# Hand-placed attention units and shared output parts in a fused attention + SwiGLU kernel

## The chip, the cores and the metric

One core of one Trainium2 chip. The metric is device time in microseconds (us) of one execution. Most executions of one kernel agree within a per cent (the four of before: 264.87 to 266.14); those that are over 1.5% above the fastest of the same kernel are marked slow and left out of the ratios.

The engines by their names in the profile: PE is the matrix engine (TensorE), PEld its weight loads, DVE the vector engine, ACT the scalar engine, POOL GpSimd, SP the sync engine, which here issues DMAs; SPq is its queue.

## The reference

Sliding-window attention with sink tokens, followed by RMS norm and a SwiGLU feed-forward network (FFN), on 4 x 768 tokens. Cut to what matters:

```python
# q, k, v: (4 batches, 8 heads, 768 positions, 64), float32; n_sink = 4, window = 128
keep = is_sink | ((rel >= 0) & (rel < window))            # rel = query position - key position
a = softmax(where(keep, q @ k.T / sqrt(64), -1e9))
x = concat_heads(a @ v)                                   # (3072, 512)

xn = x / sqrt(mean(x * x) + 1e-6) * rms_g
g  = xn @ w_gate                                          # (512, 1536)
out = (g * sigmoid(g) * (xn @ w_val)) @ w_out             # (1536, 512), float32 out
```

## The kernel before

The 3072 tokens are 24 blocks of 128 (6 for each batch), and 6 *groups* of 4 blocks. The FFN runs a group at a time. Its work is a list of *parts*: for each of 12 slices of the hidden size one gate part and one value part (four matmuls of 512 columns each), then 12 output parts of four matmuls (three for each of the group's four blocks). So a whole group has 36 parts. One part takes PE 0.863 us by the spacing of its matmuls in the trace.

Between the parts the kernel sets *attention units* of blocks to come. For block g these are, in order: scores (`unit_s`), the product with v (`unit_attend`), and for every second block an RMS chain (`unit_rms`: eight small DVE operations) that ends in two scaled blocks `xr`. From block 8 on a DMA transpose issued on SP makes `xnt` of `xr`, the layout that gate and value matmuls read. The first matmul of a group reads the `xnt` of all four of its blocks, so the last one has a deadline. From block 12 on q and k are transposed by DMA too (`qkT`), on the same SP queue. Loads of q, k, v are issued on POOL.

```python
def parts_f(G, fts, cols):
    def gate():                     # PE: pg ; ACT: th = tanh(pg / 2)
        ...
    def val():                      # PE: pvl ; DVE: p = (th + 1) * pg ; DVE: hT = p * pvl
        ...
    return [gate, val]

def parts_o(G, tb):                 # three parts; each: 4 matmuls po += hT * wo
    ...

# unit_av, the end of unit_attend:
    later(1 if g < GB else 2, lambda: unit_sq(g, u))        # ACT: sum of squares
    if u == 1 and g >= 2 and g % 2 == 1:
        later(2 if g < GB else 4, lambda: unit_rms(g))      # DVE chain, after so many parts

# the end of unit_rms:
    for i in range(2):
        unit_xr(g - 1 + i, y[:, 5, i:i + 1])                # DVE xr, then SP DMA transpose to xnt

# the driver (GB = 4 blocks a group, NG = 6 groups): units spread evenly over a group's parts
def run(parts, slots):
    n, i = len(parts), 0
    for s, f in enumerate(parts):
        while i < len(slots) and i < (s + 1) * len(slots) / n:
            for u in slots[i]:
                u()
            i += 1
        f()
        tick()                      # runs what `later` has put off

for G in range(NG):
    parts = fb[8:] if G == 0 else []
    if G > 0:
        for ft in range(FTN):
            parts += parts_f(G, (ft,), slice(0, GN))
        for tb in range(GB):
            parts += parts_o(G, tb)
    n1 = 4 * ((G + 2) * GB + 1 - 4) + (3 if G == 0 else 4)
    run(parts, slots[n:n1])
    n = n1
# [cut: prologue, attention units, loads]
```

The softmax here doesn't subtract the row's maximum and nothing guards it: scores larger than these inputs give would overflow.

## Time and profile before

| kernel before | |
|---|---|
| time, median of 4 runs | 264.96 us (264.87 to 266.14) |
| profiled execution (a run of its own, 267.6 us) | span 265.6 us, mean granted clock 0.972 |
| first gate matmul of groups 0 to 5, end of the last matmul | 17.1, 76.0, 118.2, 156.5, 195.8, 230.3, 261.6 us |
| stretches at half clock | 15.0-21.8, 35.5-38.9, 107.2-110.6 us |

First the profile page of before: busy time of each engine, the granted clock in 40 slices of the span (tenths), the chain of waits by engine, and one of the costliest groups (busy us, mean ns of one; then the idle time before its instructions, and what ended most of it).

```profile
PE 244.9 (92%) x1735; PEld 124.3 (47%) x1761; DVE 167.9 (63%) x398; ACT 139.0 (52%) x322; POOL 106.1 (40%) x145
...
PEclk9968979999999999799999999999999999999998
...
PE 58%; DVE 28%; ACT 8%; issue 4%; DMA 1%; DVEq 0%; ACTq 0%
...
L669 PE MATMUL po<-wo,hT 128*128 128x512 bf16 x279 | 66.5, 385 | 6.6 <-DVE hT L654 6.0
```

PE is the engine that bounds, but its 92% is not how close to the end it is: the matmul of 512 columns is listed at 385 ns, and four of them follow each other in 863 ns, 216 ns each, so the listed times overlap. Waits below are read from the spacing of matmuls: the start of one, less the start of the one before and what that one takes undisturbed.

The idle time of 6.0 us in the last line is the place where the change aims. The timeline of DVE and then of PE at the end of group 3 (start us, duration us, engine, line, operation, output<-inputs, form, count; in brackets the idle time before and what ended it):

```profile
180.35 0.69 DVE L654 TENSOR_TENSOR hT<-p,pvl 128x512 bf16<-128x512 bf16 x1
180.95 0.15 DVE L541 SCALAR_TENSOR_TENSOR m<-ms 128x2 f32<-128x2 f32 x1
...
182.00 0.16 DVE L563 SCALAR_TENSOR_TENSOR y<-y 128x2 f32<-128x2 f32 x1
182.20 1.41 DVE L578 SCALAR_TENSOR_TENSOR xr<-x,y,gb 128x512 bf16<-128x512 bf16 x2
183.53 0.68 DVE L646 SCALAR_TENSOR_TENSOR p<-th,pg 128x512 bf16<-128x512 bf16 x1
184.32 0.69 DVE L654 TENSOR_TENSOR hT<-p,pvl 128x512 bf16<-128x512 bf16 x1
```

```profile
181.26 2.54 PE L669 MATMUL po<-wo,hT 128*128 128x512 bf16 x11
185.06 0.39 PE L669 MATMUL po<-wo,hT 128*128 128x512 bf16 x1 [1.27 <-DVE hT L654]
```

The RMS chain and two `xr` (180.95 to 183.6) stand on DVE ahead of the last `p` and `hT`; PE has run 11 output matmuls and waits for that `hT`. The SP queue, in the same stretch:

```profile
182.98 2.50 SPq L585 DMA_TRANSPOSE xnt<-xr  x2
```

The last two transposes for group 4 are issued at 183.0 and 184.3.

### The profile page before, as it was taken

How to read it: one execution, taken by the hardware profiler on the slowest of the kernel's cores; microseconds unless marked ns; L12 is line 12 of the kernel's file. 1: busy time of each engine (PE TensorE's matmuls, PEld its weight loads, DVE VectorE, ACT ScalarE, POOL GpSimd, SP SyncE). 2: the span in 40 equal slices, each digit the busy share in tenths (PEclk: the TensorE clock that was granted, in tenths of full speed). 3: DMA queues.
4: the chain of work that ended last, by engine and by line, in shares of the span. 5: the costliest groups of instructions: out<-in, count | busy, mean ns of one | idle time of the engine just before them, and what ended most of it. 6: DMA issues, size and time to landing. Idle time of an engine off the chain costs nothing.

```text
span 265.6 us, 4787 instructions
## 1 busy us (share of the span) xinstructions
PE 244.9 (92%) x1735; PEld 124.3 (47%) x1761; DVE 167.9 (63%) x398; ACT 139.0 (52%) x322; POOL 106.1 (40%) x145
## 2 busy tenths in 40 slices
PE   7989879998999996999998998998999998999993
PEld 2546658554544442444443443443444443444441
DVE  4644757796658988317979139988139984078700
ACT  2748644789985551645662464571664431333211
POOL 8977787378999850742321100330331000000000
PEclk9968979999999999799999999999999999999998
DMA  9999999998999999696410640501221103200022
GB/s 128 153 175 191 182 155 190 174 155 88 160 148 178 141 146 87 109 158 111 88 33 20 140 121 21 83 20 33 88 79 39 3 0 80 99 22 0 0 81 79
DMA packets 108025, 26.27 MB, mean 99 GB/s; under 512 B 97249, under 2 KB 104929, under 8 KB 108002
## 3 DMA queue, kind: packets, MB, share of 16 engines
q0 software_dynamic: 80704, 13.90, 70.3%
q1 hardware_dynamic: 26258, 11.81, 21.6%
q10 hardware_dynamic: 1040, 0.26, 0.5%
q8 instruction: 14, 0.23, 0.4%
q14 instruction: 9, 0.07, 0.1%
HBM read 28.31 MB, written 6.29 MB: 130 GB/s over the span
## 4 chain that ended last, share of the span: by engine, by line
PE 58%; DVE 28%; ACT 8%; issue 4%; DMA 1%; DVEq 0%; ACTq 0%
PE po L669 17%; PE pg L628 16%; PE pvl L628 15%; DVE hT L654 7%; DVE p L646 6%; DVE xr L578 5%; ACT et L443 2%; PE pT L434 2%; ACT th L641 2%; DVE x L522 2%; PE pqk L241 2%; DVE et L409 2%; DMA osb<-in_q_dram 1%; PE pv L487 1%; PE pv L483 1%
## 5 line engine op out<-in xcount | busy, mean ns | idle before, releaser
L628 PE MATMUL pg<-xnt,wg 128*128 128x512 bf16 (+1 forms) x310 | 75.2, 364 | 3.2 <-ACT xnt L617 1.2
L628 PE MATMUL pvl<-xnt,wv 128*128 128x512 bf16 (+1 forms) x314 | 74.6, 362 | 0.4 <-DVE p L646 0.2
L641 ACT ACTIVATE th<-pg 128x512 bf16<-128x512 f32 x72 | 43.4, 602 | 56.6 <-PE pg L628 54.2
L669 PE MATMUL po<-wo,hT 128*128 128x512 bf16 x279 | 66.5, 385 | 6.6 <-DVE hT L654 6.0
L646 DVE SCALAR_TENSOR_TENSOR p<-th,pg 128x512 bf16<-128x512 bf16 x72 | 49.2, 683 | 27.6 <-ACT th L641 27.1
L654 DVE TENSOR_TENSOR hT<-p,pvl 128x512 bf16<-128x512 bf16 x72 | 49.5, 687 | 10.2 <-PE pvl L628 2.0
L411 POOL TENSOR_SCALAR_AFFINE_SELECT et<-et 128x512 bf16<-128x512 bf16 x30 | 19.5, 656 | 85.8 <-ACT et L443 77.9
L628 PEld LDWEIGHTS <-wg 128*128 128x128 bf16 x320 | 31.0, 100 | 32.4 <-issue 3.5
L669 PEld LDWEIGHTS <-hT 128*128 128x128 bf16 x288 | 27.7, 99 | 39.3 <-DVE hT L654 8.0
L628 PEld LDWEIGHTS <-wv 128*128 128x128 bf16 x320 | 31.4, 100 | 30.1 <-issue 0.3
L443 ACT ACTIVATE et<-pT 128x512 bf16<-128x512 f32 x76 | 39.4, 607 | 1.4 <-PE pT L434 1.4
L676 ACT ACTIVATE osb<-po 128x512 f32<-128x512 f32 x24 | 14.4, 600 | 47.2 <-PE po L669 47.2
L517 DVE RECIPROCAL rden<-pv 128x4 f32<-128x4 f32 x48 | 8.4, 176 | 32.5 <-PE pv L487 32.5
L123 POOL DMA_DIRECT2D v<-in_v_dram x24 | 21.8, 910 | 4.5 <-DMA wo<-in_moe_w_out_dram 2.8
L110 POOL DMA_DIRECT2D ks<-in_k_dram x23 | 20.8, 905 | 4.0 <-DMA wo<-in_moe_w_out_dram 3.1
L110 POOL DMA_DIRECT2D qs<-in_q_dram x23 | 20.9, 908 | 3.1 <-DMA wv<-in_moe_w_val_dram 2.1
L522 DVE TENSOR_TENSOR x<-pv,rden 128x256 bf16<-128x256 f32 x48 | 20.4, 424 | 1.7
L532 ACT ACTIVATE sq<-x 128x256 bf16<-128x256 bf16 x48 | 20.0, 431 | 2.0 <-DVE x L522 1.1
L416 POOL TENSOR_SCALAR_AFFINE_SELECT et<-et 128x512 bf16<-128x512 bf16 x24 | 16.0, 667 | 0.0
L578 DVE SCALAR_TENSOR_TENSOR xr<-x,y,gb 128x512 bf16<-128x512 bf16 x20 | 14.9, 785 | 0.4
L487 PE MATMUL pv<-v,et 128*128 128x65 bf16 x168 | 12.7, 194 | 1.2 <-DVE et L409 0.8
L434 PE MATMUL pT<-qkT 64*128 64x256 bf16 (+1 forms) x168 | 12.5, 262 | 0.4 <-DVE p L646 0.4
(79 smaller groups left out, 185.7 us busy)
## 6 DMA issues: line engine op xcount, KB each, us to landing
out_dram<-osb SPq DMA_DIRECT2D x24, 256.0 KB, 2.2
v<-in_v_dram POOLq DMA_DIRECT2D x24, 128.0 KB, 7.1
qs<-in_q_dram POOLq DMA_DIRECT2D x23, 128.0 KB, 6.5
ks<-in_k_dram POOLq DMA_DIRECT2D x23, 128.0 KB, 6.9
wg<-in_moe_w_gate_dram POOLq DMA_DIRECT2D x6, 256.0 KB, 8.1
wv<-in_moe_w_val_dram POOLq DMA_DIRECT2D x6, 256.0 KB, 8.2
wo<-in_moe_w_out_dram POOLq DMA_DIRECT2D x2, 768.0 KB, 11.3
osb<-in_q_dram SPq DMA_DIRECT2D x1, 256.0 KB, 3.9
```

The lines of the kernel that those rows point to most:

```text
L110: nc.gpsimd.dma_start(out=tl, in_=src[b, :, t * P:(t + 1) * P, :].rearrange("h t d -> t h d"),)
L123: nc.gpsimd.dma_start(out=V16[b][:, t, :, 0:D], in_=v[b, :, t * P:(t + 1) * P, :].rearrange("h t d -> t h d"),)
L411: nc.gpsimd.affine_select(out=ev[:, :, 0, :], in_=ev[:, :, 0, :], compare_op=ALU.is_ge, fill=0.0, base=0, pattern=[[0, x], [1, P]], channe ...
L443: nc.scalar.activation(out=et[:, hi].rearrange("p j n c -> p (j n c)"), in_=banks[u][hi], func=ACT.Exp, scale=inv_sqrt_d,)
L522: nc.vector.tensor_tensor(out=X16[g][:, heads_of(g, u), :], in0=pvv[:, :, 0:D], in1=RDEN.pop((g, u)).unsqueeze(2).to_broadcast((P, 4, D)), ...
L532: nc.scalar.activation(out=sq, in_=xh, func=ACT.Square, scale=MS_SCALE, accum_out=MS[g // 2][:, g % 2, u:u + 1],)
L578: nc.vector.scalar_tensor_tensor(out=xr, in0=x16, scalar=y, in1=gb, op0=ALU.mult, op1=ALU.mult,)
L628: nc.tensor.matmul(out=ps[:, i * n:(i + 1) * n], lhsT=w_sb[:, kt, ft * P:(ft + 1) * P], rhs=XNT[G][:, kt, cols], start=(kt == 0), stop=(kt ...
L641: nc.scalar.activation(out=st["th"], in_=st["pg"], func=ACT.Tanh, scale=0.5)
L646: nc.vector.scalar_tensor_tensor(out=p1, in0=st["th"], scalar=1.0, in1=st["pg"], op0=ALU.add, op1=ALU.mult,)
L654: nc.vector.tensor_tensor(out=HT[key][:, i:i + n, cols], in0=p1.rearrange("p (n c) -> p n c", n=n), in1=pvl.rearrange("p (n c) -> p n c", ...
L669: nc.tensor.matmul(out=st["po"], lhsT=HT[(G, ft // 2)][:, ft % 2, tb * P:(tb + 1) * P], rhs=wo[:, ft, :], start=(ft == 0), stop=(ft == FTN ...
```

## The change

Its intent: (1) fewer waits in the prologue and group 0; (2) half of a group's output parts (9 of group 0's 12 stay, 6 of the others') go between the gate and value parts of the *next* group, to thin out DVE's work there; (3) attention units at hand-picked part numbers; (4) the RMS chain in three pieces (chain, xr, xr), each put off to another part, so that the last `hT` does not wait for them. The diff, cut to its core:

```diff
-        ps = pp[0].tile([P, 512], FP32, name="pgt", tag="ph", bufs=6)   # unit_gb: RMS weights spread by
-        ...                                                             # one-row fp32 matmuls
+    nc.sync.dma_start(out=gt, in_=moe_rms_g.rearrange("(k p) -> p k", p=P))
+    # and gb by a broadcast DMA; more idle (warming) matmuls in the prologue
@@ masks of group 1's blocks on POOL, not DVE
-            dve = b < POOL_MASK_FROM or t == 0
-            wait = 0 if not dve else 1 if g < GB else 1 + 2 * u
+            wait = 0 if not by_dve(g) else 1 if g < GB else 1 + u
@@ unit_av, unit_rms
-            later(1 if g < GB else 2, lambda: unit_sq(g, u))
+            later(0 if g < GB else 1, lambda: unit_sq(g, u))
-            later(2 if g < GB else 4, lambda: unit_rms(g))
+            later(0 if g < GB else 1 if g < 2 * GB else 3, lambda: unit_rms(g))
-            unit_xr(g - 1 + i, y[:, 5, i:i + 1])
+            later(0 if g < GB else 1 if g < 2 * GB else 1 + i, lambda i=i: unit_xr(g - 1 + i, y[:, 5, i:i + 1]))
@@ loads, a group later
-    LOADS = {4: (8, 9), 5: (10, 11), 6: (12,), 7: (13, 14), 8: (15,), 9: (16, 17),
-             10: (18,), 11: (19, 20), 12: (21,), 13: (22, 23)}
+    LOADS = {8: (13, 14), 9: (15,), 10: (16, 17), 11: (18,), 12: (19, 20), 13: (21,),
+             14: (22, 23)}
@@ the driver: [cut: hand-picked part numbers for group 0]
+                for ft in range(FTN):
+                    parts += parts_f(G, (ft,), slice(0, GN))
+                    if ft % 2 == 1 and outs:
+                        parts.append(outs.pop(0))
+                for g in range(8 if G == 1 else 4 * G + 5, min(4 * G + 9, NB + 1)):
+                    p = 5.5 * (g - 8) if G == 1 else 9 * (g - 4 * G - 5)
+                    slots += step(g, p, 1.4 if g < 12 else 2)
+            outs = [p for tb in range(GB) for p in parts_o(G, tb)]
+            own = 9 if G == 0 else 6 if G < NG - 1 else len(outs)
+            parts += outs[:own]
+            outs = outs[own:]
```

`step(g, p, d)` puts the four stages of block g's units at parts p, p+d, p+2d, p+3d. It also attends block g - 1.

More of the change, by code (lines that the diff above doesn't have):

```diff
@@ L69 @@
     FA = 8
-    POOL_MASK_FROM = 1
     MANUAL = {mybir.EngineType.PE, mybir.EngineType.SP, mybir.EngineType.Pool}
@@ L154 @@
     nc.vector.memset(sel, 0.0)
-    raw = [opool.tile([P, DM], FP32, name="osb") for _ in range(3)]
+    raw = [opool.tile([P, DM], FP32, name="osb") for _ in range(2)]
     for i, src in enumerate((q, k)):
@@ L163 @@
         )
-    nc.sync.dma_start(
-        out=raw[2][0:1, :], in_=moe_rms_g.rearrange("(o d) -> o d", o=1),
-    )
-    nc.vector.memset(gb[0:1, 0:P], 1.0)
+    nc.sync.dma_start(out=gt, in_=moe_rms_g.rearrange("(k p) -> p k", p=P))
     def unit_cast(i):
@@ L172, in unit_cast @@
         (QS, KS_)[i][0] = tl
-    def unit_gb():
-        ps = pp[0].tile([P, 512], FP32, name="pgt", tag="ph", bufs=6)
-        for kt in range(KTN):
-            nc.tensor.matmul(
-                out=ps[:, kt:kt + 1], lhsT=raw[2][0:1, kt * P:(kt + 1) * P],
-                rhs=gb[0:1, 0:1], start=True, stop=True, skip_group_check=True,
-            )
-        nc.scalar.copy(out=gt, in_=ps[:, 0:KTN])
-        ps = pp[0].tile([P, 512], FP32, name="pgb", tag="ph", bufs=6)
-        nc.tensor.matmul(
-            out=ps, lhsT=gb[0:1, 0:P], rhs=raw[2][0:1, :], start=True, stop=True,
-        )
-        nc.scalar.copy(out=gb, in_=ps)
     with tc.manual_schedule(engines={mybir.EngineType.Pool, mybir.EngineType.DVE}):
@@ L231 @@
             load_v(g)
+            if g == GB + 1:
+                nc.gpsimd.memset(gb, 0.0)
         load_q(2 * GB)
+        load_k(2 * GB)
         load_wo(0)
@@ L254, in unit_t1 @@
             QKT[b] = qkt.tile([P, 2, HP, S], BF16, name="qkT")
-        ps = pp[0].tile([P, 512], FP32, name="pqk", **kind(g == 2)).bitcast(BF16)
+        ps = pp[0].tile([P, 512], FP32, name="pqk", **kind(False)).bitcast(BF16)
         transposes(ps, (QS, KS_)[i].pop(g), 0)
@@ L264, in unit_load @@
             load_q(g)
-        load_k(g)
+            load_k(g)
         load_v(g)
@@ L401, in bank, with by_dve, mask @@
         return pp[0].tile([P, 512], FP32, name="pT", tag="b1")
-    def mask(ev, b, t, nq):
+    def by_dve(g):
+        return g < GB or g % NT == 0
+    def mask(ev, g, nq):
         x = ev.shape[1]
-        if b < POOL_MASK_FROM or t == 0:
+        t = g % NT
+        if by_dve(g):
             m = masks[:, 0 if t == 0 else 1, 0:nq, :]
@@ L453, in masked @@
                 e = et if len(his) == 2 else et[:, his[0]:his[0] + 1]
-                mask(e.rearrange("p i j n c -> p (i j) n c"), b, t, nq)
-            dve = b < POOL_MASK_FROM or t == 0
-            wait = 0 if not dve else 1 if g < GB else 1 + 2 * u
+                mask(e.rearrange("p i j n c -> p (i j) n c"), g, nq)
+            wait = 0 if not by_dve(g) else 1 if g < GB else 1 + u
             for his in [(0, 1)] if nq == 2 else [(0,), (1,)]:
@@ L595, in unit_x @@
         xr = XR.pop(g)
-        n = KTN // 2 if g < GB else KTN
+        n = KTN // 2 if g < 2 else KTN
         for k0 in range(0, KTN, n):
@@ L608, in unit_x @@
                 nc.scalar.copy(out=dest, in_=src)
-            elif k0 > 0:
+            elif k0 > 0 or g == 3:
                 nc.vector.tensor_tensor(
@@ L680, in parts_o, with step @@
         return [lambda i=i: part(i) for i in range(FTN // 4)]
-    LOADS = {4: (8, 9), 5: (10, 11), 6: (12,), 7: (13, 14), 8: (15,), 9: (16, 17),
-             10: (18,), 11: (19, 20), 12: (21,), 13: (22, 23)}
-    def step(g):
+    LOADS = {8: (13, 14), 9: (15,), 10: (16, 17), 11: (18,), 12: (19, 20), 13: (21,),
+             14: (22, 23)}
+    def step(g, p, d):
         b, t = divmod(g, NT)
+        at = [p + d * i for i in range(4)]
         slots = [[], [], [], []]
@@ L695, in step @@
                 slots[1].append(lambda: unit_sink(b))
-        if GB < g <= NB:
+        if 2 * GB < g <= NB:
             slots[0].append(lambda: unit_attend(g - 1))
-        if g - 2 < NB and g % 2 == 1 and GB <= g - 3:
-            slots[1].append(lambda: unit_x(g - 3))
-            slots[2].append(lambda: unit_x(g - 2))
-        if GB + 2 <= g + 2 < NB and not by_dma(g + 2):
-            slots[2 if t != 5 else 1].append(lambda: unit_t(g + 2))
+        if g + 2 < NB and not by_dma(g + 2):
+            slots[2].append(lambda: unit_t(g + 2))
         if g + 4 < NB and by_dma(g + 4):
@@ L706, in step @@
             slots[3].append(lambda l=l: unit_load(l))
-        return slots
+        return [(x, u) for x, us in zip(at, slots) for u in us]
     def run(parts, slots):
-        n, i = len(parts), 0
+        slots = sorted(slots, key=lambda e: e[0])
         for s, f in enumerate(parts):
-            while i < len(slots) and i < (s + 1) * len(slots) / n:
-                for u in slots[i]:
-                    u()
-                i += 1
+            while slots and slots[0][0] <= s:
+                slots.pop(0)[1]()
             f()
             tick()
+        assert not slots
     with tc.manual_schedule(engines=MANUAL_ALL):
@@ L742 @@
         unit_sq(1, 0)
-        unit_warm(1)
+        unit_warm(2)
         unit_av(1, 1)
@@ L746 @@
         unit_sq(1, 1)
-        unit_gb()
         unit_rms(1)
-        unit_warm(4)
+        unit_warm(11)
         unit_x(0)
@@ L753 @@
         unit_t1(2, 1)
+        unit_warm(1)
         nc.vector.tensor_scalar(
@@ L762 @@
         PROLOGUE[0] = False
+        nc.sync.dma_start(
+            out=gb, in_=moe_rms_g.rearrange("(o d) -> o d", o=1).to_broadcast((P, DM)),
+        )
     with tc.manual_schedule(engines=MANUAL_ALL):
@@ L772 @@
             fb += parts_f(0, (ft,), slice(0, GN))
-        for tb in range(GB):
-            fb += parts_o(0, tb)
         run(fa, [
-            [],
-            [lambda: unit_bias(1, 1), lambda: unit_sp(1, 1), lambda: unit_sink(0)],
-            [lambda: unit_t1(3, 0)],
-            [lambda: unit_s(2), lambda: unit_t1(3, 1)],
-            [lambda: unit_sink_scores(0, 2), lambda: unit_bias(3, 0), lambda: unit_sp(3, 0), lambda: unit_attend(2)],
-            [lambda: unit_attend(3)],
-            [],
-            [lambda: unit_t1(4, 0)],
+            (1, lambda: unit_bias(1, 1)),
@@ L784 @@
+            (1, lambda: unit_sp(1, 1)),
+            (1, lambda: unit_sink(0)),
+            (2, lambda: unit_t1(3, 0)),
+            (3, lambda: unit_s(2)),
+            (3, lambda: unit_t1(3, 1)),
+            (4, lambda: unit_sink_scores(0, 2)),
+            (4, lambda: unit_bias(3, 0)),
+            (4, lambda: unit_sp(3, 0)),
+            (4, lambda: unit_attend(2)),
+            (5, lambda: unit_attend(3)),
+            (7, lambda: unit_t1(4, 0)),
         ])
         run(fb[:8], [
-            [lambda: unit_bias(3, 1), lambda: unit_x(2), lambda: unit_sp(3, 1), lambda: unit_x(3)],
@@ L787 @@
-            [],
-            [],
-            [lambda: unit_t1(4, 1)],
-            [],
-            [],
-            [lambda: unit_t1(5, 0)],
-            [lambda: unit_t1(5, 1)],
-        ])
-        slots = []
-        for g in range(4, NB + 3):
-            slots += step(g)
-        n = 0
+            (0, lambda: unit_bias(3, 1)),
+            (0, lambda: unit_sp(3, 1)),
+            (0, lambda: unit_x(2)),
+            (0, lambda: unit_x(3)),
+            (3, lambda: unit_t1(4, 1)),
+            (6, lambda: unit_t1(5, 0)),
@@ new lines @@
+            (7, lambda: unit_t1(5, 1)),
+        ])
+        first = [
+            (0, lambda: unit_sink_scores(0, 4)),
+            (0, lambda: unit_s(4)),
+            (1, lambda: unit_t(6)),
+            (1, lambda: unit_load(8)),
+            (1, lambda: unit_load(9)),
+            (2, lambda: unit_s(5)),
+            (2, lambda: unit_attend(4)),
+            (3, lambda: unit_t(7)),
+            (5, lambda: unit_s(6)),
+            (5, lambda: unit_attend(5)),
+            (6, lambda: unit_t(8)),
+            (6, lambda: unit_load(10)),
+            (8, lambda: unit_s(7)),
+            (8, lambda: unit_attend(6)),
+            (9, lambda: unit_sink(1)),
+            (9, lambda: unit_x(4)),
+            (10, lambda: unit_x(5)),
+            (10, lambda: unit_load(11)),
+            (13, lambda: unit_load(12)),
+            (12, lambda: unit_attend(7)),
+            (15, lambda: unit_t(9)),
+            (16, lambda: unit_x(6)),
+            (16, lambda: unit_x(7)),
+        ]
@@ L799 @@
+        outs = []
         for G in range(NG):
-            parts = fb[8:] if G == 0 else []
-            if G > 0:
+            if G == 0:
+                parts, slots = fb[8:], first
+            else:
+                parts = []
                 for ft in range(FTN):
                     parts += parts_f(G, (ft,), slice(0, GN))
-                for tb in range(GB):
-                    parts += parts_o(G, tb)
-            n1 = 4 * ((G + 2) * GB + 1 - 4) + (3 if G == 0 else 4)
-            run(parts, slots[n:n1])
@@ L808 @@
-            n = n1
+                    if ft % 2 == 1 and outs:
+                        parts.append(outs.pop(0))
+                slots = []
+                for g in range(8 if G == 1 else 4 * G + 5, min(4 * G + 9, NB + 1)):
[3 more added lines that the diff above has]
+            own = 9 if G == 0 else 6 if G < NG - 1 else len(outs)
@@ L810 @@
+            parts += outs[:own]
+            outs = outs[own:]
+            run(parts, slots)
 _INS = ['q', 'k', 'v', 'n_sink', 'window', 'moe_w_gate', 'moe_w_val', 'moe_w_out', 'moe_rms_g']
```

## The prediction

> **What bounds the kernel now.** TensorE. The page gives PE 92% busy, the chain of waits 58% PE, 28% DVE. [...]I read spacing in the timeline: four 512-column matmuls take 0.863 us, 864 of them 186 us. With attention's matmuls (about 35 us after the prologue), a 16 us prologue and the 4 us tail the floor is near 242 us; the span is 265.6. The 23 us above it:
>
> - Granted clock 0.5 in 15.0-21.8, 35.5-38.9 and 107.2-110.6, costing about 2.4, 1.3 and 1.7 us. [...] The first follows the one-row fp32 matmuls for the RMS weights (11.4-13.3).
> - 33.9 and 36.1: 1.3 us each; PE waits for the RMS chain, xr and the eviction of blocks 2, 3.
> - Rest of group 0: 0.7 (DVE mask), 1.6 (QK eviction, 62-65), 0.6.
> - Output parts: PE does 11 po matmuls (2.4 us), then waits for the last hT: 2.4 us at 106, 1.4 at 146, 185, 222. The DVE timeline shows why: RMS chain (1.25) and two xr (1.4) sit ahead of the last p and hT.
> - Mid-group PSUM/DVE waits: 0.6 at 88, 0.6 at 127, 1.6 at 165-167.
>
> **What the change does.** It
> 1. fills the prologue's wait with warming matmuls, RMS weights by DMA;
> 2. runs the chain of blocks 2, 3 at once, evicts one on ACT, one on DVE;
> 3. moves group 0's later masks from DVE (0.65 us each) to POOL;
> 4. puts half the output parts between the next group's gate/value parts, where DVE (12 x 1.37 us FFN plus about 11 us attention a group) was as loaded as PE;
> 5. splits chain/xr/xr, after the last hT in groups 2 on.
>
> **Sum, critical path only.** First gate matmul at 16.2 instead of 17.1; full clock; second half of group 0 begins at 32.1 instead of 36.1 (1 us lost to block 2's masked scores), less half clock: -4.6. Rest of group 0: -2.0. Group 1: -4.5. Groups 2-4: -4.3 at output starts, -2.2 inside. Given back +3.5: the chain now begins after the last hT, so the next group's fourth xnt lands late (transpose 2.4 us to landing, 1.2-1.3 us of SP issue each, in order). At group 3's start two QK transposes stand between xnt(14) and xnt(15): about 2 us; at group 5, with no attention at its start, about 1. Net -14.
>
> **Prediction: 251 us, 8 in 10 within 246.5 to 256.** Faster by over 2%: 0.96; within 2%: 0.03; slower: 0.01.
>
> **What would show it.** Clock 1.0 over 5-30 us, mean above 0.985; po's waits for hT (6.0 us) under 1 us; tail still 4 us; gate matmuls waiting on the xnt transpose at the starts of groups 3 and 5 only; groups 2 and 3 of about 37 us, first gate to first gate, against 38.3 and 39.3.
>
> **What would make it wrong.** Group 0 now reaches the DMA stream, whose landings do not move: the second wo half, at 51.3 now, lands at about 53 behind a K block and the RMS broadcast, just when the first output parts want it; a wait costs one for one. POOL masks queue behind DMA issues. [...] The clock could still halve at 30-36.

The terms above come to -14.1, the net of -14. That shorter waits would keep the clock full ("full clock", "less half clock") was my estimate from the stretches at half clock in the trace of before; nothing had shown it then.

## The result, and the profile after

| | before | changed |
|---|---|---|
| time, median | 264.96 us | 276.5 us (275.28 to 277.53, 4 runs) |
| ratio to before | | 1.042 (95%: 1.037 to 1.048): slower |
| profiled span, mean granted clock | 265.6 us, 0.972 | 273.4 us, 0.975 |
| first gate matmul of groups 0 to 5, end of the last matmul | 17.1, 76.0, 118.2, 156.5, 195.8, 230.3, 261.6 | 17.6, 71.1, 113.0, 156.1, 197.4, 233.1, 269.5 |
| half clock | 15.0-21.8, 35.5-38.9, 107.2-110.6 | 35.1-38.5, 113.6-117.0, 154.6-161.4 |

Ratios here and below are the mean time of one kernel's fast runs over that of the other's fast runs of the same rounds, so not quite the ratio of the medians that I quote. The profiles understate the loss: the profiled execution of before had three half-clock stretches and a clock of 0.972, while 18 of the 21 executions of before in the experiments had 0.984 to 1.000; the four executions of the changed kernel had 0.963 to 0.975.

Output parts moved between groups (three out of group 0, three net out of group 1, six into group 5, 0.863 us each). With that taken out, the difference of 7.9 us at the last matmul is, to 0.1: start +0.5, group 0 -2.8, group 1 +2.3, group 2 +4.8, group 3 +2.1, group 4 +1.1, group 5 0.0. Even the gain of group 0 is partly an illusion: about 2 us of it is attention of block 8 that now runs in group 1.

The page of the changed kernel, with the lines that answer to those of before and one more (gate matmuls):

```profile
PE 246.5 (90%) x1760; PEld 123.9 (45%) x1760; DVE 165.8 (61%) x392; ACT 139.7 (51%) x320; POOL 110.2 (40%) x152
...
PEclk9999979999999999899999869999999999999999
...
PE 65%; DVE 16%; ACT 5%; DMA 5%; issue 3%; POOL 3%; SPq 2%; DVEq 0%; ACTq 0%
...
L616 PE MATMUL pg<-xnt,wg 128*128 128x512 bf16 (+1 forms) x320 | 77.3, 370 | 13.6 <-issue 3.9
...
L657 PE MATMUL po<-wo,hT 128*128 128x512 bf16 x288 | 67.9, 379 | 1.6 <-DVE hT L642 1.6
```

The wait that the change aimed at fell from 6.0 to 1.6 us. A new one took its place: gate matmuls were idle 13.6 us, against 3.2 before, and the chain now holds 5% DMA and 2% SP queue, where it had 1% and none. The view of waits, its lines for gate matmuls (total us, times, longest):

```profile
PE pg L616 <- issue: 3.9, 1, 3.9
PE pg L616 <- DMA xnt<-xr: 3.9, 1, 3.9
...
PE pg L616 <- DVE xnt L598: 2.7, 1, 2.7
```

The first of these is put down to "issue", but it is the same wait: it ended at 113.03, and the last `xnt` of that group landed at 112.94. By spacing, gate matmuls wait 4.1 us at the start of group 2, 4.0 at group 3, 1.6 at group 4 and 1.15 at group 5, together 10.8 us; before had no such wait in those four places. Here is group 3's, in the timelines of DVE, SP and PE:

```profile
145.93 0.69 DVE L642 TENSOR_TENSOR hT<-p,pvl 128x512 bf16<-128x512 bf16 x1
146.54 0.15 DVE L529 SCALAR_TENSOR_TENSOR m<-ms 128x2 f32<-128x2 f32 x1
...
147.78 1.41 DVE L566 SCALAR_TENSOR_TENSOR xr<-x,y,gb 128x512 bf16<-128x512 bf16 x2
```

```profile
148.56 1.19 SPq L573 DMA_TRANSPOSE xnt<-xr  x1
149.84 2.31 SPq L262 DMA_TRANSPOSE qkT<-qs  x1
152.24 1.22 SPq L262 DMA_TRANSPOSE qkT<-ks  x1
153.55 1.22 SPq L573 DMA_TRANSPOSE xnt<-xr  x1
```

```profile
145.04 6.21 PE L657 MATMUL po<-wo,hT 128*128 128x512 bf16 x28
...
156.13 1.87 PE L616 MATMUL pg<-xnt,wg 128*128 128x512 bf16 x4 [3.85 <-DMA xnt<-xr]
```

The last `hT` is done first, as intended, and the output matmuls run through. But the chain comes only after it, both `xr` are ready at 149.2, and the last transpose waits on SP until 153.55 because two q/k transposes stand ahead of it. It lands at 156.0; PE had nothing to do from 152. And then those four gate matmuls take 1.87 us instead of 1.02, since the clock has halved.

How much cover the last transpose had, in both traces:

| last `xnt` for group | 2 | 3 | 4 | 5 |
|---|---|---|---|---|
| before: issued, group's first gate matmul | 105.2, 118.2 | 145.5, 156.5 | 184.3, 195.8 | 221.6, 230.3 |
| cover | 13.0 | 11.0 | 11.5 | 8.7 us |
| changed: issued, first gate matmul | 107.7, 113.0 | 153.6, 156.1 | 193.5, 197.4 | 230.5, 233.1 |
| cover (all of it needed: it landed at) | 5.3 (112.9) | 2.5 (156.0) | 3.9 (197.3) | 2.6 (233.0) us |

The reason stands in the part numbers. Before, `unit_attend` of group 3's last block (15) ran at part 18 of group 2's 36, and its chain after part 22. In the changed kernel the evenly stepped p = 0, 9, 18, 27 begins with block 12, so block 15 is attended at part 27, a quarter of a group later. Its chain comes after part 29 and its two `xr` after parts 30 and 31. That is about seven parts, 6 us, and an attention unit less between the chain and the deadline.

One more view shows what a wait costs beyond itself. The windows view of the changed kernel gives busy us (and instructions) for PE, PEld, DVE, ACT and POOL, then the granted clock, then DMA engines busy and GB/s. The stretches are 3.413 us long, laid end to end on a grid on which all its half-clock stretches begin (35.1, 113.6 and 154.6 lie 23.0 and 35.0 such lengths from the first):

```profile
31.69:35.10 3.41, 0.66 (x10) 0.46 (x8) 2.77 (x5) 1.87 (x6) 2.21 (x4) 1.00 2.06 200
35.10:38.51 3.41, 3.41 (x19) 2.41 (x17) 1.16 (x2) 0.60 (x1) 2.89 (x4) 0.50 2.43 155
103.37:106.78 3.41, 1.85 (x10) 0.75 (x9) 2.34 (x4) 0.60 (x1) 0.00 (x0) 1.00 2.80 149
110.19:113.60 3.41, 0.57 (x3) 0.32 (x4) 0.00 (x1) 0.59 (x2) 3.41 (x6) 1.00 0.81 232
113.60:117.02 3.42, 3.42 (x17) 1.50 (x15) 1.55 (x4) 2.04 (x7) 1.32 (x2) 0.50 1.55 146
151.15:154.57 3.42, 1.13 (x27) 0.82 (x26) 1.12 (x4) 1.57 (x3) 1.22 (x2) 1.00 0.41 79
154.57:157.98 3.41, 1.85 (x5) 0.74 (x6) 0.00 (x0) 0.00 (x0) 0.00 (x0) 0.50 0.81 230
195.53:198.94 3.41, 2.01 (x23) 1.09 (x21) 1.12 (x4) 2.24 (x5) 2.39 (x4) 1.00 0.49 156
```

Here the grid stretches in which PE was busy a third of the time or less (0.66, 0.57, 1.13 of 3.41) were followed by one at half clock; those with 1.85 and 2.01 were not. So half clock came after the waits at groups 2 and 3 and not after the shorter one at group 4; d_warm, below, tests whether these waits set it off. (The stretch at 154.57, itself at half clock with the end of the wait in it, has 1.85 too and is followed by more half clock.) In before, on its own grid (half clock from 35.50 and 107.18), it shows too; the two lines left out are those stretches at half clock:

```profile
32.09:35.50 3.41, 1.69 (x20) 0.86 (x19) 3.10 (x13) 1.52 (x5) 1.68 (x3) 1.00 2.41 156
...
103.77:107.18 3.41, 1.21 (x19) 0.72 (x19) 2.07 (x4) 0.75 (x2) 0.00 (x0) 1.00 0.38 77
...
182.27:185.68 3.41, 2.14 (x15) 0.86 (x14) 2.63 (x4) 0.19 (x1) 0.00 (x0) 1.00 0.24 50
```

This is probably also why executions of the same kernel differ: the grid does not begin with the kernel (its first line is at 0.97 us in the changed kernel's span and at 1.37 in before's), and the same wait, cut in two by a grid line, may pass. The trace of b_order, a run below, has the very wait of group 0 that half clock follows here (31.76 to 34.73); there a grid line falls at 32.8, PE is busy 1.47 of the next 3.41 us, and no half clock follows. In both traces of this section every change of the granted clock lies on its grid of 3.413 us. The stretch ahead of a change to half clock was not always mostly idle: one half busy (1.69 of 3.41, before, 32.1-35.5) was followed by half clock, though one of the changed kernel as busy (1.73, 14.6-18.0) and b_order's, busy less, were not. The share alone does not decide in between (the figures of all traces stand in the last section).

### The profile page after: what moved, and what is told of

It reads as the page before. It is cut to its first block, busy times and chain, and to the rows that moved or that the text cites. A ratio compares the mean times of both kernels' runs of the same rounds, so it can differ in the third digit from the quotient of the medians.

```text
span 273.4 us, 4816 instructions
## 1 busy us (share of the span) xinstructions
PE 246.5 (90%) x1760; PEld 123.9 (45%) x1760; DVE 165.8 (61%) x392; ACT 139.7 (51%) x320; POOL 110.2 (40%) x152
## 4 chain that ended last, share of the span: by engine, by line
PE 65%; DVE 16%; ACT 5%; DMA 5%; issue 3%; POOL 3%; SPq 2%; DVEq 0%; ACTq 0%
PE pg L616 20%; PE pvl L616 19%; PE po L657 16%; DMA xnt<-xr 4%; DVE hT L642 4%; DVE xr L566 3%; DVE p L634 3%; ACT et L432 2%; PE pT L423 2%; DMA osb<-in_q_dram 2%; DVE x L510 1%; DVE et L398 1%; PE pqk L226 1%; PE pv L475 1%; SPq L262 1%
## 5 line engine op out<-in xcount | busy, mean ns | idle before, releaser
L616 PE MATMUL pg<-xnt,wg 128*128 128x512 bf16 (+1 forms) x320 | 77.3, 370 | 13.6 <-issue 3.9
L616 PE MATMUL pvl<-xnt,wv 128*128 128x512 bf16 (+1 forms) x320 | 76.7, 368 | 0.5 <-DVE hT L642 0.5
L657 PE MATMUL po<-wo,hT 128*128 128x512 bf16 x288 | 67.9, 379 | 1.6 <-DVE hT L642 1.6
L400 POOL TENSOR_SCALAR_AFFINE_SELECT et<-et 128x512 bf16<-128x512 bf16 x34 | 22.0, 656 | 99.4 <-ACT et L432 92.7
L664 ACT ACTIVATE osb<-po 128x512 f32<-128x512 f32 x24 | 14.4, 599 | 34.0 <-PE po L657 33.9
L405 POOL TENSOR_SCALAR_AFFINE_SELECT et<-et 128x512 bf16<-128x512 bf16 x26 | 17.0, 653 | 0.0
```

What stands on the lines that cost most here:

```text
L400: nc.gpsimd.affine_select(out=ev[:, :, 0, :], in_=ev[:, :, 0, :], compare_op=ALU.is_ge, fill=0.0, base=0, pattern=[[0, x], [1, P]], channe ...
L616: nc.tensor.matmul(out=ps[:, i * n:(i + 1) * n], lhsT=w_sb[:, kt, ft * P:(ft + 1) * P], rhs=XNT[G][:, kt, cols], start=(kt == 0), stop=(kt ...
L657: nc.tensor.matmul(out=st["po"], lhsT=HT[(G, ft // 2)][:, ft % 2, tb * P:(tb + 1) * P], rhs=wo[:, ft, :], start=(ft == 0), stop=(ft == FTN ...
```

## The experiments

The theory, after reading the traces: the chain comes too late for the next group's first matmul (**placement**), and two things make it worse: q/k transposes ahead of the last `xnt` on SP (**order**) and a burst of loads beside it (**loads**); each wait of about 4 us then costs half clock (**clock**). Rivals: the output parts themselves, moved between gate and value parts, cost the time (**interleaving**); the new prologue does (**prologue**); putting the chain off with three pieces alone does (**chain**). All kernels compute the reference's result within tolerance. Each batch ran on one chip with its own runs of before, so compare ratios, not medians across batches. Four runs each; of these two are marked slow in a_loads and in b_order, one in g_chain and in j_space. The medians here are over all four, the ratios over the fast ones.

| run | batch | median us | before us | ratio to before (95%) |
|---|---|---|---|---|
| a_loads | 1 | 276.63 | 265.29 | 1.033 (1.023 to 1.044) |
| b_order | 1 | 268.17 | 265.29 | none: two of four runs slow |
| d_warm | 1 | 268.76 | 265.29 | 1.012 (1.005 to 1.019) |
| e_prologue | 1 | 265.33 | 265.29 | 0.999 (0.992 to 1.005) |
| f_own12 | 2 | 265.29 | 265.63 | 1.001 (0.995 to 1.006) |
| g_chain | 2 | 267.44 | 265.63 | 1.005 (0.998 to 1.012) |
| h_both | 2 | 265.28 | 265.63 | 1.001 (0.996 to 1.006) |
| i_best1 | 2 | 257.94 | 265.63 | **0.972** (0.968 to 0.977) |
| j_space | 3 | 263.18 | 264.73 | 0.992 (0.984 to 1.000) |
| k_g0 | 3 | 261.38 | 264.73 | 0.988 (0.983 to 0.994) |
| l_best2 | 3 | 258.24 | 264.73 | 0.976 (0.969 to 0.984) |
| m_own12 | 3 | 260.37 | 264.73 | 0.984 (0.978 to 0.991) |

### a_loads: loads elsewhere

```diff
-    LOADS = {8: (13, 14), 9: (15,), 10: (16, 17), 11: (18,), 12: (19, 20), 13: (21,),
-             14: (22, 23)}
+    LOADS = {8: (13, 14, 15), 9: (16, 17), 10: (18,), 13: (19, 20), 14: (21,), 15: (22,),
+             16: (23,)}
```

> The changed kernel with group 1's loads of q, k, v blocks 13 to 18 issued some 10 us earlier and none of 19, 20 before group 2. In the changed kernel xnt(10) took 7.8 us from issue (103.8) to landing (111.6), while loads were landing until 111.4. Theory L (the load burst, moved a group later by the change, delays the last transposes of group 1): the wait of the first gate matmul of group 2 falls from 4.1 us to under 1.5, the half clock after it (3.4 us long) goes, and the time falls by 4 to 6 us against the changed kernel (276.5), to about 271.5; the wait at group 3 (4.0) stays. Rival Q (order on the SP queue: QK transposes between the last two xnt): group 2's wait stays near 4 us and the time within 1 us. Rival C (too few output parts left at a group's end to cover the chain): the wait stays at 3 us or more.

Measured: 276.63 us, 1.033 (fast runs 273.40 and 275.49): most of the loss stayed. The profile is of a run marked slow (278.49), so only waits and landings are read from it, no times. The wait at group 2 became 2.7 us by spacing, that at group 3 5.1. The SP queue of a_loads shows what was left at group 2:

```profile
108.61 1.19 SPq L573 DMA_TRANSPOSE xnt<-xr  x1
109.90 1.22 SPq L262 DMA_TRANSPOSE qkT<-qs  x1
111.21 2.59 SPq L262 DMA_TRANSPOSE qkT<-ks  x1
113.89 1.22 SPq L573 DMA_TRANSPOSE xnt<-xr  x1
```

The order keeps the last `xnt` back there: its `xr` is ready at 110.6, and it is issued 3.3 us later. At group 3 my own edit did harm: block 22's load now fell beside xnt(14), which took 7.3 us from issue to landing (151.7 to 159.0). In the changed kernel the same happened at group 2: xnt(10) was issued at 103.8 and landed at 111.6 (7.8 us), while POOL's loads landed until 111.4; in the traces of before and of the changed kernel the eight `xnt` transposes with two or more of POOL's loads in flight took 4.2 to 7.8 us to land, and of the 19 with none in flight 13 took 2.4 to 2.6 and six 3.7 to 4.6. What makes them late beside loads is not shown. Loads matter, but this run does not separate their share.

### b_order: q/k transposes of blocks 16 and 20 three parts later

```diff
+        if g in (12, 16):
+            at[2] = p + 7
```

> The changed kernel with the QK transposes of blocks 16 and 20 moved behind the last xnt of groups 1 and 2 on the SP queue, nothing else. Theory Q: at group 3's start xnt(15) is issued at about 149.8 instead of 153.6, lands by 153.5 at the latest, the wait falls from 4.0 to 0.5-1.5 us and the half clock (6.8 us long there) goes: -4.5 to -6 us, to about 271.5. Group 2's wait stays within 1 us of 4.1, because all four transposes there landed within 1.3 us of each other behind the loads. Rival C: xnt(15) is late even without them, as the chain starts after the last hT: the wait stays above 2.5 us.

Measured: 267.45, 264.74 (fast), 268.89, 271.57 (slow). The median is 8 us under the changed kernel's, but the runs scatter too far for a ratio. In its profile the two last transposes at group 3 go out back to back, and the wait there is 1.2 us instead of 4.0. The wait at group 2 stays at 3.2: there the transposes land late (109.9 and 110.3), just after loads (the last at 108.4). Order is a large part of the loss.

### d_warm: idle matmuls in the two longest waits

```diff
+            if G in (2, 3):
+                slots.append((0, lambda: unit_warm_bank(14)))   # 14 idle matmuls, 512 columns
```

> The changed kernel with 14 idle matmuls (3.0 us) put before the first gate matmul of groups 2 and 3, inside the two waits of 4 us. If the half clock after these waits is set off by the idle array, both windows (3.4 and 6.8 us) go and the time falls by 1.7 + 3 = about 4 to 5 us, to 272, while the two waits themselves still end at the same landing. If the half clock has another cause, it stays and the time is the changed kernel's within 1 us.

Measured: 268.76 us, 1.012 against 1.042 for the changed kernel: 0.030 of 265 us, 8 us. The edit makes no transpose earlier and takes no useful work away. PE at group 2 (the trace holds 13 of the 14 idle matmuls):

```profile
109.70 3.18 PE L331 MATMUL pT<-idle 128*128 128x512 bf16 x13
113.24 1.02 PE L624 MATMUL pg<-xnt,wg 128*128 128x512 bf16 x4 [0.36 <-issue]
```

Its profile has full clock in 99-125 and 145-165; one half-clock stretch is left, at 33.1-39.9 in group 0. By the profiles (273.4 and 267.0 us) group 2 is shorter by 2.7 us and group 3 by 4.0; of the latter 1.6 us is the wait at group 4, which is gone in this run, as its last `xnt` landed after 2.4 us here and 3.8 us there; of the former 1.1 us is a q/k transpose ahead of group 3's last `xnt` that took SP 1.2 us here and 2.3 there. Why these two differ is not shown. The rest, about 4 us, is the clock after the two waits, which agrees with 4.4 us, half of the half-clock time after them. So somewhat over a third of the loss of 11 us was paid after the waits, not in them. This I had priced at nothing.

### e_prologue: before, with only the new prologue

```diff
+    nc.sync.dma_start(out=gt, in_=moe_rms_g.rearrange("(k p) -> p k", p=P))
-        unit_gb()
-        unit_warm(4)
+        unit_warm(11)
[cut: the rest of the prologue's part of the change]
```

> The kernel before with the change's prologue alone (RMS weights by DMA, no fp32 matmuls, nine more warming matmuls, the broadcast gb). The prediction said -3.3 us here: gate start 16.2 for 17.1 and no half clock in 15-22. Rival: the half clock goes, but the 2 to 3 us are absorbed in the wait for blocks 2 and 3 (group 0's second half began at 34.7 in the changed kernel, 36.1 before, though the first gate matmul was 0.5 us later): within 1 us of the kernel before.

Measured: 265.33 us, 0.999. Within the interval of 0.7% the prologue is worth nothing either way, and rival **prologue** falls. Its profile has full clock in 15.0-21.8, as I predicted of the change, but the profiled execution of before was unlucky: 18 of 21 others have a mean clock of 0.984 or more, which leaves no room for all three of its half-clock stretches (13.6 us at half clock are 0.026 of the span). I had counted a run's luck as a gain.

### f_own12: all 12 output parts in their own group

```diff
-            own = 9 if G == 0 else 6 if G < NG - 1 else len(outs)
+            own = len(outs)
```

> The changed kernel with all 12 output parts of a group run at its own end again (the interleaving undone), all else kept. Theory C (six parts, 5.2 us, taken from the end of a group are the cover that the chain and its transposes had: before, the last xnt landed 7 to 11 us before the next group's first gate): the waits at the starts of groups 2 to 5 fall from 4.1, 4.0, 1.6, 1.2 to 0 (the longest is under 5.2), half clock windows there go; DVE-bound stalls inside the groups return, 1 to 3 us a group; together 266 to 270 us. Rival (interleaving pays for itself): 276 or more.

Measured: 265.29 us, 1.001; undoing the interleaving alone takes away the whole loss. On its own this would crown the rival. But its profile says how: without parts between them, the gate and value parts end five parts earlier in the list, so the chain is no longer queued behind the last `hT`. The waits at groups 4 and 5 are gone, that at group 3 falls to 2.5 (the order on SP remains: `xnt` issued at 148.2 and 152.1) and at group 2 to 1.6. So this run cannot tell "interleaving costs" from "interleaving made the late chain later". m_own12 below can.

### g_chain: chain and both xr together again, one part later

```diff
-            later(0 if g < GB else 1 if g < 2 * GB else 3, lambda: unit_rms(g))
+            later(0 if g < GB else 1 if g < 2 * GB else 4, lambda: unit_rms(g))
-            later(0 if g < GB else 1 if g < 2 * GB else 1 + i, ...)
+            later(0 if g < GB else 1 if g < 2 * GB else 0, ...)
```

> The changed kernel with the RMS chain of blocks 8 on in one piece again (chain and both xr 4 parts after the attention unit, as before), all else kept. Groups 2 on: both xnt stand ahead of the QK transposes on the SP queue, but the chain still follows the last hT: group 3's wait falls from 4.0 to 1-1.5, those of groups 4, 5 stay within 0.5 us of 1.6 and 1.2. Group 2: transposes still behind the loads, its wait stays 3 us or more; the hT wait at the end of group 1 (1.7) stays. 4 to 6 us faster than the changed kernel if theory Q holds (271-272), the same if the split is innocent.

Measured: 267.44 us, 1.005. A miss in the right direction: I expected at least 3 us of wait to stay at group 2, and 0.7 stayed. With both `xr` in one part, both transposes go out early and back to back (issued at 101.6 and 102.9); they still take 6.2 and 6.8 us to land (107.8, 109.7). The waits at groups 3 to 5 are 0.9, 1.6 and 1.2. The price is the wait for `hT` in group 1 (2.4 us). Splitting the chain opened the gap on SP that the q/k transposes fell into.

### h_both: order and loads together

```diff
+        if g in (12, 16):
+            at[2] = p + 7
-    LOADS = {8: (13, 14), 9: (15,), 10: (16, 17), 11: (18,), 12: (19, 20), 13: (21,),
-             14: (22, 23)}
+    LOADS = {8: (13, 14), 9: (15, 16), 10: (17, 18), 13: (19, 20), 14: (21, 22), 17: (23,)}
```

> b_order plus loads that land before the last transposes of groups 1 and 2 (a_loads showed 7.3 us to landing for xnt(14) where block 22's load had been moved beside it). b_order left 3.2 us at group 2 with the order right, a_loads left 2.7 with the loads gone but the order wrong: with both, the wait at group 2 falls under 0.5, at group 3 to about 1.2, groups 4 and 5 keep 1.6 and 1.2. Theory L+Q: 263 to 266 us. If the wait at group 2 stays above 2, a third cause holds it.

Measured: 265.28 us, 1.001. With order and loads mended the wait at group 2 is gone, while 1.8, 1.6 and 1.2 us stay at groups 3 to 5. The chain is still a quarter of a group late, so **placement** is what these have in common. It is not all of them: at groups 3 and 4 the last `xnt` took 4.0 and 3.9 us to land, with no load in flight. In k_g0, with the same units and loads there, group 3's took 2.4 us and the wait was 0.5. What makes one transpose land later than another here is not shown. Interleaving and the split chain are both in this kernel, and it is no slower than before.

### j_space: h_both with the units seven parts apart, not nine

```diff
-                    p = 5.5 * (g - 8) if G == 1 else 9 * (g - 4 * G - 5)
+                    p = 5 * (g - 8) if G == 1 else 7 * (g - 4 * G - 5)
```

> h_both (265.3) with nothing but the attention units moved from 9 parts apart to 7 in groups 2 on, and from 5.5 to 5 in group 1. If the chain's place after the last hT is what is left of the waits, those at groups 3, 4, 5 (1.8, 1.6, 1.2) go below 0.3 and the time falls by 4 to 5, to about 261; the hT wait at the end of group 1 (1.7) stays or grows to 2.4. If DVE then delays the last hT as in the kernel before, po waits of about 1 us a group appear and 263 to 265 is left.

Measured: 263.18 us, 0.992 (0.984 to 1.000; one of four runs slow). All waits at group starts are gone, which settles **placement**. The last block is now attended at part 21, not 27. SP ahead of group 3:

```profile
142.04 2.50 SPq L573 DMA_TRANSPOSE xnt<-xr  x2
```

The last of these lands at 145.8, and the group's first gate matmul runs at 150.0. From the first gate matmul of group 2 to the last matmul the profile has 145.5 us, against 150.1 in h_both: 4.6 us, the sum of h_both's three waits. But the whole gain is only 0.9% of the time, about 2.3 us, less than the 4 to 5 that I expected: in this profile group 0's wait of 3.1 us brought 6.8 us of half clock against 3.4 in h_both, and group 1, with its units 5 parts apart, took 40.4 us against 38.9. The wait for `hT` in group 1 stayed at 1.8.

### k_g0: h_both with group 0 mended

In group 0, the changed kernel's second half began at 34.7 us and not at the 32.1 that I had predicted. On DVE the eviction of block 3 stands behind two pairs of `p` and `hT`; the DVE timeline of the changed kernel:

```profile
31.21 0.68 DVE L634 SCALAR_TENSOR_TENSOR p<-th,pg 128x512 bf16<-128x512 bf16 x1
31.99 0.69 DVE L642 TENSOR_TENSOR hT<-p,pvl 128x512 bf16<-128x512 bf16 x1
...
33.99 0.68 DVE L598 TENSOR_TENSOR xnt<-pxt,gt 128x512 bf16<-128x512 bf16 x1
```

The experiment puts the two transposes and evictions into the last value part, ahead of its `p` and `hT`, and six idle matmuls into what is left of the wait:

```diff
+            for f in HOOK.pop((G, fts[0], cols.start), ()):    # in val(), after the matmuls
+                f()
+        HOOK[(0, 6, 0)] = (lambda: unit_x(2), lambda: unit_x(3))
-            (0, lambda: unit_bias(3, 1)),        # bias and scores move to part 7 of the first half
-            (0, lambda: unit_sp(3, 1)),
-            (0, lambda: unit_x(2)),
-            (0, lambda: unit_x(3)),
+            (0, lambda: unit_warm_bank(6)),
```

> h_both with nothing but group 0's change of i_best1 (blocks 2, 3 transposed before the p/hT pair of the last first-half part, idle matmuls in the wait). The first gate of group 0's second half at about 32.8 instead of 34.3, no half clock at 33-37: -1.5 to -3.5 us, to 262-264. j_space and k_g0 together with the order of the output parts (1.7) should account for i_best1's -7.3 against h_both.

Measured: 261.38 us, 0.988, about 3.3 us under h_both by the ratios. PE in k_g0:

```profile
31.30 0.61 PE L597 MATMUL pxt<-ident,xr 128*128 128x128 bf16 x8
31.75 1.46 PE L331 MATMUL pT<-idle 128*128 128x512 bf16 x6
33.04 1.04 PE L624 MATMUL pg<-xnt,wg 128*128 128x256 bf16 x8
```

The second half begins at 33.0 instead of 34.7 (34.3 in h_both), and no half clock follows. By the profiles group 0 accounts for 2.6 us, start included; another 1.5 lies in groups 2 to 5, where the edit changes nothing, most of it group 3's shorter wait. So here is the gain of group 0 that the prediction had counted on; the change itself did not take it.

### i_best1: everything together

j_space, k_g0, and the output parts reordered so that four of them (16 matmuls) need no late `hT`:

```diff
+            if 0 < G < NG - 1:
+                outs[:6] = [outs[i] for i in (0, 1, 3, 4, 2, 5)]
```

> h_both, with attention units 7 parts apart in groups 2 on (5 in group 1), so that the chain precedes the last two feed-forward tiles; the first two blocks' outputs of a group ordered so that 16 po matmuls, not 8, precede the first that needs the last hT; and in group 0 block 3's eviction ahead of a p/hT pair on DVE, with six idle matmuls in the wait after it. Waits at the starts of groups 2 to 5 under 0.3 each (-2.8 against h_both), the hT wait of group 1 (1.7) under 0.5, the wait at 34.7 from 2.9 to about 1.5 with no half clock. 256 to 260 us. If DVE cannot take the chain before the last hT, po waits of 1 us a group come back, and 260 to 263.

Measured: 257.94 us (257.68 to 258.19), 0.972: faster than both kernels. The page of i_best1 (its span is 256.1 us, its mean clock 1.000), then SP and PE at the start of group 3:

```profile
PEclk9999999999999999999999999999999999999999
```

```profile
136.23 2.50 SPq L581 DMA_TRANSPOSE xnt<-xr  x2
138.82 1.22 SPq L262 DMA_TRANSPOSE qkT<-qs  x1
```

```profile
144.17 1.02 PE L624 MATMUL pg<-xnt,wg 128*128 128x512 bf16 x4
```

The last `xnt` lands at 140.0, 4.2 us before it is needed. There is no wait at any group's start, no output matmul waits for `hT`, and the clock never halves. The group's four gate matmuls take 1.02 us where the changed kernel's took 1.87.

### l_best2: i_best1 with three more small moves

A mask put off by one part, ten output parts kept in group 0, evictions of blocks 6 and 7 one part later:

```diff
-            wait = 0 if not by_dve(g) else 1 if g < GB else 1 + u
+            wait = 0 if not by_dve(g) else 1 if g < 2 * GB else 1 + u
-            own = 9 if G == 0 else 6 if G < NG - 1 else len(outs)
+            own = 10 if G == 0 else 6 if G < NG - 1 else len(outs)
-            (16, lambda: unit_x(6)),
-            (16, lambda: unit_x(7)),
+            (17, lambda: unit_x(6)),
+            (17, lambda: unit_x(7)),
```

> i_best1 (257.9) with block 6's second mask one part earlier on DVE, ahead of the chain (a wait of 1.1 us at 55.3), and one more output part of group 0 at its end, so that the chain of blocks 6, 7 has 0.9 us more cover (wait of 1.0 at 65.3). Both waits under 0.3: 256.0 to 257. If other waits take their place, 257.5 or more.

Measured: 258.24 us (256.93 to 259.69), 0.976: no gain over i_best1 within the intervals.

### m_own12: i_best1 without interleaving

```diff
-            own = 9 if G == 0 else 6 if G < NG - 1 else len(outs)
+            own = len(outs)
```

> i_best1 with the interleaving undone: all 12 output parts of a group at its own end, everything else kept. What the interleaving itself is worth once the chain is in its right place: DVE again has 29 parts' work in 24 parts, so po waits for hT of 1 to 2 us a group and PSUM waits inside the groups come back; 261 to 264. If the interleaving is worth nothing, 258.

Measured: 260.37 us, 0.984, on the chip where l_best2, with interleaving, had 0.976. From first gate matmul to first gate matmul, group 2 took 37.7 us (i_best1: 37.6), group 3 37.3 (37.1), group 4 34.4 (34.5) and group 5 31.2 (31.3 after its six extra output parts are taken out). The difference of 2 us lies in group 1, where m_own12's profile has a half-clock stretch (98.0-101.4) that i_best1's lacks. Just ahead of it attention's matmuls wait 2.5 us for `p` and `hT` (94.2-96.9), against 1.7 in i_best1; whether the interleaving is what spares group 1 the half clock was not tested. I had expected 1 to 2 us of waiting for `hT` in each group. There was none; PE in m_own12, group 2:

```profile
140.25 10.52 PE L667 MATMUL po<-wo,hT 128*128 128x512 bf16 x48
```

All 48 output matmuls run through without a wait. So once the chain is placed well, interleaving is worth 0.1 to 0.2 us in each of groups 2 and 3 and nothing in 4 and 5; in group 1 it may be worth up to 2. It does not cost the time (rival **interleaving** falls), and in groups 2 to 5 it does not earn it either.

## Why the prediction was wrong

The prediction was 251 us, 246.5 to 256, and 96% for faster by over 2%. The change ran at 276.5 us.

- **The step that failed: "Given back +3.5".** I named the mechanism: the chain now begins after the last hT, the fourth xnt lands late, two QK transposes stand between xnt(14) and xnt(15). But I allowed about 2 us at group 3 and 1 us at group 5, and expected waits "at the starts of groups 3 and 5 only". The runs showed 4.1, 4.0, 1.6 and 1.15 us at groups 2 to 5, 10.8 in all. I had not counted the cover in parts: the new places move a whole attention unit a quarter of a group closer to the deadline (j_space undoes just that, on top of h_both, and every such wait is gone). I had also priced each landing at 2.4 us: at group 2 I left out loads, beside which one took 7.8 us, and at group 4 the last took 3.8, for a cause not found.
- **"Full clock" was assumed.** I named the clock halving as a risk at 30-36 only. After waits of about 4 us at groups 2 and 3 the clock was halved for 3.4 and 6.8 us; idle matmuls in just these two waits brought back 8 us by the ratios (d_warm), about 4 of it the clock's by the profiles.
- **Group 0, "second half of group 0 begins at 32.1": wrong.** It began at 34.7, because block 3's eviction stood behind two `p`/`hT` pairs on DVE, and half clock followed at 35.1-38.5. k_g0 gets the gain with another order.
- **The first gate matmul "at 16.2": wrong.** It came at 17.6, later than before's 17.1. Full clock over 5-30 us did come true, but e_prologue puts the worth of the whole prologue at zero within 0.7%, for before loses that stretch of clock in some executions only.
- **"Groups 2-4: -4.3 at output starts": right.** The waits for `hT` at groups 2 to 4 were gone. Group 1 kept 1.6 us, where I had said that all would sum to under 1.
- Added up, as an estimate: between my -14 and the profile's +7.8 lie 22 us. The waits at group starts are 7.3 of them (10.8 for 3.5), half clock after these 4.4 (half of 3.4 and of the 5.3 that came after the wait), group 0's second half 2.6 (the late first gate matmul is in this) and its half clock 1.7. The remaining 6 or so are gains in group 1 and inside the groups that did not come.
- **"-2.2 inside" the groups, and -4.5 in group 1: not shown.** Groups 2 and 3 took 43.1 and 41.3 us, not 37. They do take 37 in i_best1, but in m_own12 too, where the output parts do not thin out DVE. The argument that DVE bounds the middle of a group was not needed.
- **Right:** the tail of 4 us (3.9), and a wait of about 1 us at group 5 (1.15). The late `wo` that I feared did not bind: it landed at 52.3, and its first reader ran at 58.6.

The gains of single undoings do not add up: order alone brings 8 us by the medians (its runs scatter), undoing the interleaving 11, order and loads 11, warming 8, of a loss of 11. A plausible reason, argued from the grid and not measured one by one: each shortens a wait enough that the clock is not halved, so each collects the clock's part. Masks on POOL were never undone alone; in the changed kernel's trace PE waits 0.5 us for one, at 52.6 (POOL ran the masks there from 51.8 to 53.1, right after four load issues of 0.9 us each). What divides the loss exactly between order, loads and placement is not, since they share those waits.

## What to carry to other kernels

When units are moved by hand, take the one tile with a deadline, follow it from its last producer over the DMA queue to its first reader, and count the cover before and after the move; then look what else stands in that queue and what lands beside it. Price a wait on the matrix engine together with the half clock that it may set off (here 3.4 and 6.8 us of it after two waits of about 4 us), and try idle matmuls in the wait as a cheap test of which of the two hurts. One kernel's undoing of one part shows what that part did *there*: f_own12 alone would have blamed the interleaving, and m_own12 cleared it.

## What the traces show of the hardware

- In before and the changed kernel every change of the granted clock lies on a grid of 3.413 us (half-clock starts 23.0 and 35.0 windows of it apart in the changed kernel), and each stretch at half clock before the last matmul is one or two windows long. The window before one needn't be idle. Laid on each trace's own grid, the ten windows before the last matmul that ran at full clock with PE busy 37% or less were all followed by half clock (four of them in before and the changed kernel, 17 to 35% busy). Between 40% and 63% both happened: 50% (before, 32.1-35.5), 59% (m_own12, 94.6-98.0) and 63% (l_best2, 92.0-95.4) were followed by it, 43% (b_order, 32.8-36.2), 50% (h_both, 146.2-149.6) and 51% (changed, 14.6-18.0) were not. So the busy share, which is modelled, does not decide alone; what else does is open. Short gaps came with half clock too: two of 1.3 us (before, 33.9 and 36.1) and one of 2.9 us (changed, 34.7).
- One case against: before halved at 15.0 after a window that the profile shows 93% busy (3.16 of 3.41), part of it one-row fp32 matmuls (11.4-13.3). Whether those matter to the clock was not tested.
- What halvings in mid-kernel cost here: about 4 us of 273, 1.6%, after two waits (an estimate, worked out under d_warm).
- A small DMA transpose beside loads: 2.4 us from issue to landing at the least, 7.8 (changed, group 2) and 7.3 us (a_loads, group 3) with POOL's loads in flight, and 3.7 to 4.6 us at times with no load in flight (before and changed). One took SP 1.2 to 1.5 us to issue in 71 of 80 cases in these two traces and 1.6 to 2.9 in nine, in order.
- Two durations that I could not explain: DVE's first cast took 0.84 to 0.89 us in three traces (the changed kernel, b_order, l_best2) and 0.43 in the other eleven, of nearly the same code. POOL was issuing loads just then in both kinds. I did not settle why.
